# Five more filler matmuls after each of six mode pairs, and where the TensorE instruction fetches then fall

## The chip, the cores and the metric

The kernel runs on one core of one Trainium2 chip. The metric is device time in microseconds (us) of one execution; the profile's span, first to last instruction, is some 1.8 us shorter. All executions here are of the state that the harness calls fast.

## The reference, cut to what matters

```python
# linear attention with elu+1 features; q, k, v are 8 x 8 heads x 576 x 64
kv = einsum('bhsd,bhse->bhde', phi(k), v);  z = phi(k).sum(axis=2)
x  = (phi(q) @ kv) / (phi(q) . z + 1e-6)          # 8 x 576 x 512
# spectral mixing: 64 modes, one complex 512 x 512 weight for each
X = rfft(x, axis=1)[:, :64]
Y = X * (w_r + i w_i), mode by mode               # 64 x 2 x 1 MiB of float32 weights
u = x + irfft(Y, n=576)
out = u + relu(u @ w_ch)                          # 8 x 576 x 512 float32
```

The mode weights are 134 MB of float32 in memory, converted to bfloat16 on the way in. They set the length of the kernel.

## The kernel before: the parts that matter

The 64 modes are worked off in 32 pairs. Each pair needs two loads, one of w_r and one of w_i, into one of two buffers. GpSimd issues the load for pair p+2 when the products of pair p have read their buffer.

```python
def w_load(p, half, pool, tag, bufs):
    if half == 0:
        w_in[p] = pool.tile([128, NDW, D], BF16, tag=tag, bufs=bufs, name=f"w{p}")
    two = (moe_w_r, moe_w_i)[half][2 * p : 2 * p + 2]
    pin(nc.gpsimd.dma_start(out=w_in[p][half::2], in_=two.rearrange(...)))

def keep_warm(n):                       # a filler: a matmul whose result nobody reads
    for _ in range(n):
        pin(nc.tensor.matmul(last_ps[0], id16, wch16[:, 0, :]))

def mode_pair(p):
    w = w_get(p)                        # from pair 5 on: two buffers
    ...
    for dc in range(NDW):               # 16 products, wait for both loads
        product(P, xz[p % 2][:, dc]..., 32, w, dc, NDW)
    if p + 1 < LAST:
        set_diagonal(p + 1)
    st = evacuate(p, P)                 # VectorE or ScalarE
    work_slot(p, "mid")                 # other work, spread over the pairs
    picks(2 * p, st, 2)
    if p % 4 == 3:
        ...                             # VectorE moves a finished octet of modes
    work_slot(p, "end")
    keep_warm(FILL.get(p, 0))

FILL = {**{p: 7 for p in range(18, 27)}, 27: 9, 28: 5, 29: 6, 30: 4}
... # cut: attention, transforms, inverse transform and the output, see the whole kernel
```

After pair 30 comes the last pair. Its last loads arrive in pieces, each multiplied as soon as it is there (the tile y_last). The rows that come of it are copied into YZ_all by DMA, and the inverse transform, the rectifier, the sum and the stores follow from there.

Of the kernel before, what the change touches and what calls it, by code (L numbers as in the profile page):

```python
# [43 lines left out]
def kernel(  # L44
# [370 lines left out]
    def keep_warm(n: int):  # L415

        for _ in range(n):
            pin(nc.tensor.matmul(last_ps[0], id16, wch16[:, 0, :]))  # L418
# [4 lines left out]
    def work_slot(p: int, name: str):  # L423
        for _ in range(slots.get((p, name), 0)):
            if work:
                work.pop(0)()
# [34 lines left out]
    def mode_pair(p: int):  # L461
# [19 lines left out]
        work_slot(p, "end")  # L481
        keep_warm(FILL.get(p, 0))

# [47 lines left out]


    n_early = n_keep + n_pre
    FILL = {**{p: 7 for p in range(18, 27)}, 27: 9, 28: 5, 29: 6, 30: 4}
    ystage = ctx.enter_context(tc.tile_pool(name="ystage", bufs=1, side="right"))
    inv_sb = ystage.tile([2 * NM, S], F16, name="inv_sb")
    inv2_sb = ystage.tile([128, S], F16, name="inv2_sb")
# [474 lines left out]
```

## Time and profile before

| | before |
|---|---|
| time, median of the first 3 executions | 421.37 us (421.35 to 421.74) |
| span of the profiled execution | 419.6 us |
| TensorE busy, instructions traced | 288.7 us, 3115 matmuls and 3115 weight loads |
| last weight landing | 387.97 us |
| last y_last product ends | 388.27 us |
| last store landed | 418.41 us |

The page cuts the span into 40 slices of 10.5 us. The digits are tenths: TensorE's busy share, its granted clock, and the busy share of the DMA engines.

```profile
PE   0359799899517553444343685998798878899993
PEclk9999958989655555555555589799899989999997
DMA  8999999999999999999999999999999999998698
```

The DMA row is nines from the second to the 36th slice: a stream that never pauses. TensorE's clock is halved from the 12th to the 23rd slice, where it has little to do. The change puts fillers into part of that stretch.

A DMA transfer runs on 16 engines, and the trace has one landing record for each. The spread between the first and the last of the 16 tells how far the slowest engine is behind.

### The profile page before, as it was taken

How to read it: one execution, taken by the hardware profiler on the slowest of the kernel's cores; microseconds unless marked ns; L12 is line 12 of the kernel's file. 1: busy time of each engine (PE TensorE's matmuls, PEld its weight loads, DVE VectorE, ACT ScalarE, POOL GpSimd, SP SyncE). 2: the span in 40 equal slices, each digit the busy share in tenths (PEclk: the TensorE clock that was granted, in tenths of full speed). 3: DMA queues.
4: the chain of work that ended last, by engine and by line, in shares of the span. 5: the costliest groups of instructions: out<-in, count | busy, mean ns of one | idle time of the engine just before them, and what ended most of it. 6: DMA issues, size and time to landing. Idle time of an engine off the chain costs nothing.

```text
span 419.6 us, 7400 instructions
## 1 busy us (share of the span) xinstructions
PE 288.7 (69%) x3115; PEld 155.9 (37%) x3115; DVE 228.6 (54%) x499; ACT 154.2 (37%) x253; POOL 58.1 (14%) x100
## 2 busy tenths in 40 slices
PE   0359799899517553444343685998798878899993
PEld 0247677787301221222121232433343324354421
DVE  4587979994404462464645353454455433512794
ACT  4677888954101011000000233344253422230782
POOL 4222224210001111111111111111111111130000
PEclk9999958989655555555555589799899989999997
DMA  8999999999999999999999999999999999998698
GB/s 219 211 212 216 210 221 206 229 206 222 222 217 212 213 223 211 216 222 209 220 220 205 225 220 205 225 215 209 224 217 208 225 216 209 223 205 162 230 395 328
DMA packets 17073, 93.17 MB, mean 222 GB/s; under 512 B 2112, under 2 KB 3024, under 8 KB 12880
## 3 DMA queue, kind: packets, MB, share of 16 engines
q0 software_dynamic: 12496, 81.48, 93.3%
q1 hardware_dynamic: 4544, 11.22, 7.2%
q8 instruction: 24, 0.39, 0.3%
q14 instruction: 9, 0.07, 0.0%
HBM read 163.93 MB, written 9.44 MB: 413 GB/s over the span
## 4 chain that ended last, share of the span: by engine, by line
DMA 65%; PE 19%; DVE 5%; issue 3%; ACT 3%; POOL 2%; DVEq 0%; ACTq 0%; POOLq 0%
DMA w<-in_moe_w_i_dram 52%; DMA pick_sb<-row_pick 8%; PE P L431 7%; DMA k<-in_k_dram 5%; PE acc L747 3%; PE acc L787 2%; PE kvp L256 2%; ACT ke L207 2%; POOL w L116 2%; PE eps L688 1%; DVE x L292 1%; DVE ke L220 1%; POOL w L128 1%; DVE k L214 1%; PE zl L418 0%
## 5 line engine op out<-in xcount | busy, mean ns | idle before, releaser
L431 PE MATMUL P<-w,xz 128*32 128x512 bf16 x496 | 48.3, 530 | 64.3 <-DMA w<-in_moe_w_i_dram 61.8
L448 ACT CAST ys<-P 128x512 f16<-128x512 f32 x15 | 8.8, 585 | 131.6 <-PE P L431 131.6
L116 POOL DMA_DIRECT2D w<-in_moe_w_r_dram x31 | 17.8, 575 | 244.2 <-PE P L431 240.7
L431 PEld LDWEIGHTS <-xz 128*32 128x32 bf16 x496 | 13.2, 115 | 85.5 <-DMA w<-in_moe_w_i_dram 56.9
L446 DVE CAST ys<-P 128x512 f16<-128x512 f32 x17 | 11.8, 691 | 53.5 <-PE P L431 53.5
L688 PE MATMUL eps<-wch,xTw 128*128 128x512 f16 x144 | 40.6, 409 | 0.0
L162 PEld LDWEIGHTS <-qT 64*128 64x128 f16 (+1 forms) x640 | 22.8, 124 | 31.7 <-issue 17.2
L671 ACT CAST x16w<-x_main 128x512 f16<-128x512 f32 x32 | 19.8, 618 | 37.7 <-DVE x_main L669 37.7
L669 DVE TENSOR_TENSOR x_main<-ya,x_main 128x512 f32<-128x512 f32 x32 | 22.0, 691 | 18.7 <-PE ya L665 18.5
L256 PE MATMUL kvp<-vpad,ke 32*128 32x130 f16 x576 | 23.3, 255 | 9.1 <-ACT qT L243 6.4
L441 DVE COPY xz<-xt_c 64x256 bf16<-64x256 bf16 x62 | 22.9, 370 | 12.1 <-PE P L431 11.3
L696 ACT CAST E<-eps 128x512 f16<-128x512 f32 (+1 forms) x40 | 21.2, 539 | 19.5 <-PE eps L688 19.5
L256 PEld LDWEIGHTS <-ke 32*128 32x128 f16 x576 | 21.4, 113 | 10.8 <-issue 8.9
L162 PE MATMUL nw<-kv,qT 64*128 64x65 f16 (+1 forms) x320 | 18.9, 240 | 9.5 <-DVE x_tail L632 4.5
L418 PE MATMUL zl<-wch,id 128*128 128x512 f16 x93 | 23.0, 380 | 0.0
L292 DVE TENSOR_TENSOR x<-num,rd 128x512 f16<-128x512 f32 x32 | 22.1, 692 | 1.1
L236 PE MATMUL qTp<-id,qe 128*128 128x128 f16 x144 | 14.3, 278 | 11.7 <-DVE qe L220 9.5
L632 DVE TENSOR_TENSOR x_main<-nw,rd 128x256 f32<-128x256 f32 x32 | 11.2, 417 | 17.3 <-PE nw L162 17.3
L207 ACT ACTIVATE qe<-q 128x1152 f16<-128x1152 f16 (+1 forms) x16 | 17.9, 1157 | 7.5 <-DMA q<-in_q_dram 7.4
L454 PE MATMUL yt<-pick_sb,ys 128*128 128x32 f16 (+1 forms) x128 | 8.8, 186 | 16.9 <-DMA pick_sb<-row_pick 10.7
L680 DVE COPY xTw<-xTp 128x512 f16<-128x512 f16 x36 | 15.0, 416 | 10.0 <-PE xTp L678 9.9
L243 ACT COPY qT<-qTp 128x1152 f16<-128x1152 f16 x16 | 19.6, 1291 | 0.5 <-PE qTp L236 0.2
(118 smaller groups left out, 494.6 us busy)
## 6 DMA issues: line engine op xcount, KB each, us to landing
w<-in_moe_w_r_dram POOLq DMA_DIRECT2D x31, 1024.0 KB, 12.5
w<-in_moe_w_i_dram POOLq DMA_DIRECT2D x31, 1024.0 KB, 16.7
out_dram<-x_main SPq DMA_DIRECT2D x12, 512.0 KB, 3.8
k<-in_k_dram POOLq DMA_DIRECT2D x8, 576.0 KB, 13.1
v<-in_v_dram POOLq DMA_DIRECT2D x8, 576.0 KB, 14.4
q<-in_q_dram POOLq DMA_DIRECT2D x7, 576.0 KB, 12.8
out_dram<-x_main SPq DMA_DIRECT2D x8, 256.0 KB, 3.8
q<-in_q_dram SPq DMA_DIRECT2D x2, 576.0 KB, 4.5
```

The source lines that it names most:

```text
L116: nc.gpsimd.dma_start(out=w_in[p][half::2], in_=two.rearrange("g (r dc) e -> (g r) dc e", dc=NDW))
L162: mm = nc.tensor.matmul(num[hpo][orow, c0 : c0 + 65], qT[rows, hpp, h2, cols], kv_sb[rows, hpp, h2, :])
L207: pin(nc.scalar.activation(out=ev[:, c], in_=heads(nm, b, c), func=AF.Exp))
L256: nc.tensor.matmul(kv_ps[:, h2, 0:130], phi["k", b][r0 : r0 + 32, j // NJ, j % NJ].rearrange("p o d -> p (o d)"), vp[r0 : r0 + 32, :, j, 0 ...
L292: nc.vector.tensor_tensor(out=dst.rearrange("p (o c d) -> p o c d", o=2, c=4), in0=nv[:, :, :, 0:64], in1=rden.unsqueeze(3).broadcast_to([ ...
L418: pin(nc.tensor.matmul(last_ps[0], id16, wch16[:, 0, :]))
L431: nc.tensor.matmul(P[c : c + n, :], x, w[:, dc, :], start=(dc < NDC), stop=(dc >= n_dc - NDC), tile_position=(0, c), skip_group_check=True,)
L441: pin(nc.vector.tensor_copy(out=xz[p % 2][HALVES[h], :, h, :], in_=src))
L669: pin(nc.vector.tensor_tensor(out=x, in0=acc, in1=x, op=ALU.add))
L671: pin(nc.scalar.copy(out=x16w[t], in_=x))
L688: nc.tensor.matmul(e_ps, xT[:, c, :], wch16[:, c, :], start=(c == 0), stop=(c == NDC - 1))
L696: pin(nc.scalar.copy(out=dst, in_=e_ps[:, cols]))
```

## The change

The intent is in the title: 30 more fillers, five after each of the pairs 5 to 10 (modes 10 to 21). They need 60 more TensorE instructions (a weight load with each matmul), so every later 256-instruction block of TensorE's program is fetched that much earlier in the work.

```diff
-    FILL = {**{p: 7 for p in range(18, 27)}, 27: 9, 28: 5, 29: 6, 30: 4}
+    FILL = {**{p: 5 for p in range(5, 11)}, **{p: 7 for p in range(18, 27)}, 27: 9, 28: 5, 29: 6, 30: 4}
```

## The prediction

> **What bounds the kernel now.** I read the page's slices first, then sums by window, then the chain of waits over the stage that is changed, then the landing records of the single transfers. The times before are 421.35 to 421.74 us, median 421.37, and the profiled execution spans 419.6 us.
>
> The windows cut the run at the stages. The columns are busy time of each engine with its instruction count, then the granted TensorE clock, the DMA share and GB/s.
>
> ```profile
> 112.00:136.00 24.00, 10.34 (x96) 3.15 (x96) 6.32 (x15) 1.17 (x2) 2.23 (x4) 0.50 1.03 214
> 144.00:231.00 87.00, 37.54 (x474) 17.40 (x475) 43.98 (x148) 4.25 (x10) 9.78 (x18) 0.50 1.01 216
> 250.00:378.00 128.00, 106.59 (x772) 48.43 (x772) 55.42 (x114) 46.03 (x85) 16.86 (x31) 0.95 1.01 216
> 378.00:392.00 14.00, 13.15 (x126) 6.86 (x127) 5.24 (x12) 2.97 (x7) 1.11 (x2) 1.00 0.62 121
> 392.00:418.00 26.00, 20.45 (x109) 5.85 (x107) 21.24 (x21) 17.68 (x33) 0.00 (x0) 0.93 1.00 381
> ```
>
> From 144 to 231 us, the stage that the change touches, TensorE is busy 37.54 of 87 us at half clock. From 250 to 378 it is busy 106.59 of 128 us at 0.95 of the clock. The DMA share is 1.01 and the rate 216 GB/s in both. So the pace up to 378 us is the weight stream's, whatever TensorE's clock. The chain of waits says the same for this stage (start, length, what):
>
> ```profile
> 156.55 16.61 DMA w<-in_moe_w_i_dram
> 173.16 0.04 issue
> 173.21 1.93 PE P L431 x16
> 175.13 0.29 issue
> 175.42 0.54 POOL w L116
> 175.96 16.63 DMA w<-in_moe_w_i_dram
> ```
>
> A mode pair's 16 products start when its second load has landed (173.21), their end lets GpSimd issue the load two pairs ahead, and that takes 16.63 us because the other buffer's load is ahead of it. Two pairs take 19.4 us, one 9.7. With one load always still queued, shortening the 1.93 us of products issues the next load earlier but does not make the stream faster.
>
> The list of waits gives TensorE's slack:
>
> ```profile
> PE P L431 <- DMA w<-in_moe_w_i_dram: 61.8, 20, 5.8
> ```
>
> In the changed stage it idles 2.98 to 5.77 us ahead of each of the pairs 7 to 11, and 3.37 us ahead of pair 6.
>
> **Why instruction fetches could matter.** The queue table shows them:
>
> ```profile
> q0 software_dynamic: 12496, 81.48, 93.3%
> q1 hardware_dynamic: 4544, 11.22, 7.2%
> q8 instruction: 24, 0.39, 0.3%
> q14 instruction: 9, 0.07, 0.0%
> ```
>
> Queue 8 has 24 packets of 16,384 bytes. In the trace their starts follow TensorE's instruction count: 246 at the first, then about 256 apart (4310 at the 17th, 5869 at the 23rd, 6063 at the 24th). So they are TensorE's. Each takes 0.89 to 1.04 us on one DMA engine, and their durations repeat in a cycle of eight, so I infer that they go round eight engines.
>
> Each transfer posts 16 landings, and I read the time between the first and the last. It is 0.4 us up to 25 us, 1.5 after fetch 1, 2.6 after fetch 9 (94.61 us) and 3.7 after fetch 17 (255.23 us). The fetches between those bring other engines up to the slowest and add almost nothing to the last landing. So the first fetch of each round of eight costs the stream about 1.05 us and the other seven cost nothing. At the end of the loads (last landing 387.97 us) the slowest engine is 3.76 us behind the fastest.
>
> **What the Trainium skill says.**
> - "Runtime: NRT & Kernel Launch", section "Instruction fetch mechanics": instructions come in 16 KiB blocks of 256 by a DMA of the sequencer's own, TensorE holds 128 KiB, and a block crossing is mostly hidden. The trace agrees on block size and spacing. It shows no TensorE gap that a fetch ended, but a hidden cost of about 1 us per round in the weight stream.
> - "DMA: Bandwidth & Descriptors", section "Why a DMA increments its semaphore by 16 and not by 1": the 16 engines finish independently, and only the full 16 mean landed. The trace agrees (spreads of 0.4 to 3.8 us), so a wait is for the slowest engine.
> - "TensorE: Matmul & The Clock Gate", section "What's actually happening": the clock is halved unless TensorE was busy through a window of about 3.4 us. The trace agrees roughly: one unbroken half-clock stretch of 133 us, from 111 to 244 us, where TensorE has gaps of 3 to 6 us.
>
> **The change part by part.**
> 1. Added: 5 matmuls in each of the pairs 5 to 10, 30 in all. The order of instructions shows 6292 rows on TensorE against 6232, 60 more (a weight load with each), none more on another engine, and no transfer more.
> 2. Their time: the group of fillers, id times wch into zl, shows seven in 1.69 us at full clock, so five take 1.2 us, and at half clock at most 2.4. They come after a pair's other work, and the least wait after them is 2.98 us (ahead of pair 7). Left over: 0.6 us or more. They are wholly hidden: 0 us on the path.
> 3. The clock: busy time per pair goes from about 4.2 to 6.0 or 6.6 us of 9.7. That may give some full-clock windows between 145 and 195 us. Products then take 1.05 us (as at 290.65) in place of 1.90. The load two pairs ahead is issued 0.85 us earlier into a queue that holds another 9.7 us pair: 0 us.
> 4. Shifted fetches: fetch 13 comes about 30 instructions earlier in the work, fetch 14 some 50 or 60, all later ones 60, half a pair. Fetch 17 moves from 255 to about 251 us, fetch 23 from 381.95 to about 379. Both are in the stream before and after. Fetch 17 costs its 1.05 us either way, and fetch 23 nothing, as its engine was 1.2 us ahead of the slowest. There is no extra round: a 25th fetch would be due near instruction 6320 or later, and TensorE ends at 6246 plus 60.
> 5. Fetch 24, the one that changes phase: before, it starts at 396.42 us, amid the output stores (DMA share 1.00 from 392). The stores' spread goes from 0.8 to 2.0 us there. 60 instructions earlier is about 389 to 391 us, between the last weight landing (387.97) and the first stores (392), where the DMA engines are idle. Its lag of about 1.2 us on one engine is saved, but it has shrunk by the end: in the last store (418.41) three engines land 0.00, 0.09 and 0.10 us before the last, the others 0.35 to 0.53. The other two lag by what looks like queue 14's fetches at 403.53 and 407.31, which stay. So the end gains 0 to 0.1 us.
>
> The sum: 0 + 0 + 0 - 0.05 us, from 421.37 to about 421.3 us.
>
> **The rivals.**
> - Fetch 24 collides with the copy of the last rows into YZ_all. That is issued at 390.3 and 390.6 and lands at 393.54 and 394.47, and a TensorE product that reads it starts at 394.48. There is no slack, and the tail is dense on TensorE (10.00 of the 10 us from 400 to 410). A fetch at 391 to 393 on one engine could delay this by up to 1.0 us: 421.7 to 422.4. Against it: the estimate puts the fetch mostly ahead of 391. This is the main risk upward.
> - The store stream is bound by its slowest engine, not by what TensorE produces. Then moving fetch 24 away saves its whole 1.0 us: 420.4. For it: 381 GB/s and a share of 1.00 in this stage. Against it: the lag of that engine shrinks from 1.2 to about 0.4 us by itself, so the stores are waiting for data.
> - The warm clock speeds the stage. If TensorE paced the pairs, 0.85 us for each of six pairs would save 5 us: 416. Against it: pairs take 9.7 us at half clock and also at full clock (319.87 to 329.57).
> - The fillers delay products: six times 0.5 us would make 424. Against it: the slack above, and behind it the second buffer.
>
> **Range and chances.** Base 421.3. The YZ_all collision (one chance in five) adds 0.3 to 1.0 us. A store stream bound by its slowest engine (one in five) takes off 0.3 to 1.0. Runs of before spread over 0.4 us. So 420.6 to 422.0 holds 8 in 10. Two per cent is 8.4 us; none of the mechanisms with evidence reaches that.
>
> **What would show it.** Right: the same DMA share and 9.7 us per pair from 144 to 231 us. A last weight landing within 0.3 us of 387.97. 24 packets on queue 8, the 24th near 390 and the spread of the stores after 396 under 1 us. TensorE's waits ahead of the pairs 6 to 11 shorter by the fillers. Wrong: pairs longer than 9.75 us (fillers not hidden), a fourth step in the spread of landings (a 25th fetch, or a different engine), YZ_all landing after 394.6, or an end that moves with the stores' spread.

## The result, and the profile after

The changed kernel took 421.93 us (median of 6, 421.32 to 423.11). The kernel before took 421.38 us (421.28 to 421.74, 6 runs). The ratio is 1.0013, with a 95% interval of 0.9998 to 1.0027. A ratio here is the mean time of one kernel's fast runs over that of the other's of the same rounds (of the last job see below), so not quite the ratio of the medians. The verdict at 2% is "same", and the median lies in the predicted range. But it is 0.6 us above the predicted 421.3, and three of the six executions are over 422 us (long ones; those under 422 us are short). That is what the experiments are about.

First the stage that was changed. The windows have the same columns as in the prediction:

```profile
144.00:231.00 87.00, 48.57 (x499) 20.39 (x500) 44.03 (x148) 4.25 (x10) 9.76 (x18) 0.52 1.01 216
250.00:378.00 128.00, 105.80 (x762) 47.70 (x764) 55.47 (x114) 45.43 (x83) 16.81 (x31) 0.93 1.01 215
```

TensorE is busy 11 us more from 144 to 231 us, and the DMA share and the rate are what they were. The clock went from 0.50 to 0.52, one full-clock window of 3.4 us. The waits of the products for the loads between 143 and 194 us (total, count, longest) are, before:

```profile
PE P L431 <- DMA w<-in_moe_w_i_dram: 25.3, 6, 5.8
```

and after:

```profile
PE P L431 <- DMA w<-in_moe_w_i_dram: 12.2, 6, 3.6
```

13.1 us less over six pairs: the five fillers took 2.2 us a pair out of time in which TensorE waited anyway.

The fetches, from the trace, with the spread of the landings after each:

| fetch of TensorE instructions | before, us | after, us | what it did |
|---|---|---|---|
| 16 | 228.62 | 226.21 | nothing: spread 2.7, after 2.4 |
| 17, first of the third round | 255.23 | 250.31 | spread to 3.7 (before) and 3.4 (after), 1 us more in both |
| 23 | 381.95 | 379.99 | nothing on the last landing |
| 24, last | 396.42, amid the stores | 390.42, ahead of the stores | spread of the stores then 2.0 (before), 0.8 (after) |

The last weight landing is at 387.95 us, against 387.97. So the weight stream is as long as before. The span is still 0.8 us longer (420.3 against 419.6). The chain of waits says where that comes from. Before, from 371 us on (start, length, what):

```profile
371.91 14.79 DMA w<-in_moe_w_i_dram
386.71 0.05 issue
386.75 0.36 PE y_last L512 x8
387.11 0.23 PE zl L418
```

and after, the end of the same stretch:

```profile
385.37 0.59 PE P L431 x8
385.96 0.54 PE acc L787 x2
386.50 0.55 PE acc L880 x2
387.05 0.19 PE yt L454 x4
387.24 0.66 PE zl L418 x3
387.91 0.39 PE y_last L512 x16
```

Before, the chain goes back to the last load: TensorE was waiting for it. After, it goes back along TensorE alone: the pieces were there and TensorE was behind. The last y_last product ends at 389.13 us (before 388.27), and from there everything is 0.8 us later, the last store too (419.18 against 418.41). TensorE was behind because its clock was halved twice late in the run, from 351.3 to 358.1 and from 364.9 to 371.8 us. The slices show it in the clock row from the 34th to the 36th place:

```profile
PE   0369998999617775665343668888788877999993
PEclk9999998579855556555555598999999997889998
DMA  8999999999999999999999999999999999997698
```

Before, the clock was full from 342.9 to 414.6 us.

### The profile page after: what moved, and what is told of

It is laid out like the page before. It is cut to its first block, busy times and chain, and to the rows that moved or that the text cites. A ratio compares the mean times of both kernels' runs of the same rounds, so it can differ in the third digit from the quotient of the medians.

```text
span 420.3 us, 7460 instructions
## 1 busy us (share of the span) xinstructions
PE 304.5 (72%) x3145; PEld 161.2 (38%) x3145; DVE 229.5 (55%) x499; ACT 154.2 (37%) x253; POOL 57.4 (14%) x100
## 4 chain that ended last, share of the span: by engine, by line
DMA 62%; PE 26%; DVE 3%; ACT 3%; issue 2%; POOL 2%; DVEq 0%; POOLq 0%; ACTq 0%
DMA w<-in_moe_w_i_dram 49%; DMA pick_sb<-row_pick 8%; PE P L431 7%; DMA k<-in_k_dram 5%; PE acc L747 3%; PE z L710 2%; PE zl L418 2%; PE acc L787 2%; PE kvp L256 2%; POOL w L116 2%; ACT ke L207 1%; PE xf L354 1%; PE yp L723 1%; ACT qT L243 1%; PE qTp L236 1%
## 5 line engine op out<-in xcount | busy, mean ns | idle before, releaser
L431 PE MATMUL P<-w,xz 128*32 128x512 bf16 x496 | 46.9, 516 | 51.8 <-DMA w<-in_moe_w_i_dram 49.4
L418 PE MATMUL zl<-wch,id 128*128 128x512 f16 x123 | 38.9, 461 | 0.0
L688 PE MATMUL eps<-wch,xTw 128*128 128x512 f16 x144 | 38.0, 388 | 0.0
L162 PE MATMUL num<-kv,qT 64*128 64x65 f16 (+1 forms) x320 | 16.5, 219 | 5.4 <-DVE x L292 3.0
## 6 DMA issues: line engine op xcount, KB each, us to landing
w<-in_moe_w_r_dram POOLq DMA_DIRECT2D x31, 1024.0 KB, 13.1
```

Source lines behind the costliest of these rows:

```text
L162: mm = nc.tensor.matmul(num[hpo][orow, c0 : c0 + 65], qT[rows, hpp, h2, cols], kv_sb[rows, hpp, h2, :])
L431: nc.tensor.matmul(P[c : c + n, :], x, w[:, dc, :], start=(dc < NDC), stop=(dc >= n_dc - NDC), tile_position=(0, c), skip_group_check=True,)
L688: nc.tensor.matmul(e_ps, xT[:, c, :], wch16[:, c, :], start=(c == 0), stop=(c == NDC - 1))
```

## The experiments

The question: does the change slow the kernel (by its fetches or by its fillers), or did the clock, whose checks fall differently in each execution, make half of these executions late?

**The kernel before, again, as it stands.**

> The kernel before once more, unchanged, for its spread and for a second trace. Theory 1 (the clock's window, which falls differently in each execution, decides how late TensorE is at the last load): this kernel shows the same spread as the changed one if it is run often enough, so some executions of 422 us or more, and a ratio to itself of 0.999 to 1.001. Theory 2 (the change itself costs about 0.5 us): all executions stay within 421.2 to 421.8 us. Last weight landing at 387.9 to 388.1 us in the trace either way.

Measured: 424.21, 421.30, 421.55, 421.45, 421.42 and 422.22 us, ratio to its own runs 1.0011 (0.9991 to 1.0030). So the kernel before has long executions too, and compared with itself it can show about the ratio that the change showed. The profiled execution was the one of 424.21 us. Two windows of it, with the columns as before:

```profile
359.00:366.00 7.00, 6.48 (x38) 2.38 (x30) 2.84 (x5) 1.17 (x2) 1.09 (x2) 0.53 1.05 222
366.00:373.00 7.00, 7.00 (x20) 1.94 (x20) 2.40 (x5) 2.34 (x4) 0.00 (x0) 0.50 1.03 220
```

The clock was halved from 359.4 to 373.0 us. TensorE did 20 matmuls between 366 and 373 us. In the first profile of the same kernel it was:

```profile
366.00:373.00 7.00, 6.91 (x76) 4.59 (x75) 1.71 (x5) 2.93 (x5) 3.24 (x6) 1.00 1.04 220
```

76 in the same 7 us. Pair 29's products started at 373.44 us (first profile 368.39), and the last y_last product ended at 390.92 us, 2.1 us after the last landing. The span is 422.4 us, and from 378 us to the end of y_last the chain of waits runs along TensorE alone. The last landing was late too (388.81 us), so the expectation that put it at 387.9 to 388.1 in every case was wrong. The trace points to a fetch: a late TensorE fetches late, and fetch 23 came at 386.59 us (first profile 381.95). The first six pieces of the last loads landed within 0.2 us of the first profile's times, the two behind that fetch 1.0 and 0.84 us later, with the spread up from 1.1 to 2.1 us.

**The changed kernel, again.**

> The changed kernel once more, unchanged. Theory 1: a median within 0.3 us of the kernel before in the same rounds, or of its copy. Theory 2: a ratio of 1.001 to 1.002 again with an interval clear of 1. In the trace: last weight landing within 0.1 us of 387.95; if the clock is granted in full from 340 to 390 us, the last y_last product ends near 388.3 us and the span is 419.4 to 419.6; if it is halved within 340 to 375 us, it ends later and the span is longer by as much.

Measured: 421.96 us median, 421.22 to 423.27, three of six over 422; ratio 1.0014 (0.9998 to 1.0030), so not clear of 1 as theory 2 had it; but the median is 0.45 us above the 421.51 of the kernel before in these rounds, more than the 0.3 us that theory 1 allowed. Neither forecast was met. The profiled execution is a short one (span 419.8 us). Its clock was full from 255.6 to 416 us, the last landing was at 388.11 and the last y_last product ended at 388.41. With the clock up, the changed kernel is as quick as the kernel before.

**The same shift of the fetches, without the fillers' time.**

```diff
+    def small_fill(n: int):
+        for _ in range(n):
+            pin(nc.tensor.matmul(last_ps[0][0:32, 0:16], id16[:, 0:32], wch16[:, 0, 0:16]))
 ...
         keep_warm(FILL.get(p, 0))
+        small_fill(SMALL.get(p, 0))
 ...
+    SMALL = {p: 5 for p in range(5, 11)}
```

> Five matmuls of 16 columns in the place of the five fillers of 512 in each of the modes 10 to 21's pairs: the same 60 instructions and so the same shift of the fetches, but next to no TensorE time. If the shifted fetches cost something (theory 2a), this shows what the changed kernel shows, 421.9 us and the stores' spread after 396 us under 1 us. If the fillers' time and the clock do (theory 2b), it is at 421.4 us. Theory 1: 421.3 to 422 us, with fetch 24 near 389 to 391 us and nothing gained by it beyond 0.1 us.

Measured: 422.38, 421.28, 424.07, 424.06, 422.24 and 421.29 us; ratio 1.0024 (1.0001 to 1.0047). The median of 422.31 is above all three forecasts, and the interval just leaves out 1. The profiled execution was a long one: clock halved from 351.9 to 358.7 and from 365.6 to 372.4 us, last landing 387.93, TensorE 1.5 us behind at the end of y_last. Fetch 24 came at 390.97, and the stores' spread then was 0.75 to 0.9 us. The two short executions are as short as any of the kernel before. So neither the shifted fetches nor the fillers' time lengthens a short execution. The long one that was traced is of the same kind as before. Four of six is more than the kernel before has; this is taken up below.

**A fourth round of fetches inside the weight stream.** The same small matmuls, 30 after each of the pairs 6 to 14.

```diff
+    SMALL = {p: 30 for p in range(6, 15)}
```

> 270 matmuls of 16 columns, 540 instructions, spread over the pairs 6 to 14: two blocks and a little more, so that the 25th fetch, the first of a fourth round of eight engines, comes ahead of the last weight landing (near 379 us). If the first fetch of a round costs the stream 1.05 us: fetch 25 is seen before 388 us, the spread of the landings takes a fourth step to about 4.6 to 4.8 us, the last weight landing is at 388.9 to 389.1 us in place of 387.97 and the time is 422.2 to 422.6 us. If a fetch costs nothing in the stream: last landing 387.97, time 421.4 us.

Measured: fetch 25 at 381.82 us. The queue table now has

```profile
q8 instruction: 26, 0.43, 0.4%
```

and the landings read:

| weight transfer that landed last at | spread of its 16 landings |
|---|---|
| 380.69 us (before fetch 25) | 3.83 us |
| 384.05 us | 4.74 us |
| 388.91 us (the last one) | 4.59 us |

The fourth step is there, and the last landing is 0.94 us later than 387.97. In that execution TensorE was on time, and the last store landed 0.87 us later than in the first profile of before. The short ones of the six are 422.12, 422.20 and 422.47 us, as expected; three more at 423.1 to 423.7 put the median at 422.78, above what was expected; ratio 1.0029 (1.0017 to 1.0042). So in these traces a fetch's cost to the stream depends on whether its engine is already the slowest.

**Fillers where TensorE idles late, to hold the clock.** Pair 27 has waits of 0.69, 0.78 and 0.52 us inside it and 2.0 us after it.

```diff
         work_slot(p, "mid")
+        keep_warm(MID.get(p, 0))
         picks(2 * p, st, 2)
 ...
+        keep_warm(MID.get(p, 0))
         work_slot(p, "end")
 ...
+    FILL |= {24: 12, 25: 13, 26: 9, 27: 15}
+    MID = {27: 3}
```

> The kernel before, with fillers where TensorE idles between 320 and 359 us: 5 more after pair 24, 6 after 25, 2 after 26, 6 after 27, and 3 ahead of and 3 behind pair 27's picks, each set shorter than the wait that it fills (the waits are 1.75, 2.11, 0.70, 2.00, 0.69 and 0.78 us at full clock; a filler takes 0.24 us). Theory 1 (executions over 422 us come from a window of little TensorE work near 348 to 359 us, after which the clock is halved and TensorE is late at the last load): no or nearly no execution over 421.9 us, median 421.3 to 421.5 us, clock full from 345 to 390 us in the trace. Rival (the long executions come from something else, the fetches or the memory): one in four or more over 422 us as with the changed kernel, or lateness with the full clock.

Measured: 421.46 us median, five of six between 421.24 and 421.55, one of 422.34; ratio 0.9992 (0.9972 to 1.0012). The kernel before had five of eleven over 422 us in the same job (up to 424.00). The profiled execution had the full clock from 306 to 415 us.

**The same on top of the change.**

> The changed kernel (five fillers in each of the modes 10 to 21's pairs) with the same further fillers as warm_late. Theory 1: the same as warm_late within 0.2 us, all executions under 421.9 us, so that the change itself does nothing. If the shifted fetches cost something of their own: 0.3 us or more above warm_late, with long executions left.

Measured: 422.24 to 422.85 us, all six, median 422.51; ratio 1.0014 (0.9995 to 1.0034). Both theories missed this: hardly any spread, but all executions 1 us longer. The trace explains it. TensorE was on time (y_last done at 388.46, copy into YZ_all issued at 390.49, in warm_late 390.36), and yet the last store landed at 419.80 us (warm_late 418.59). The queue table has one packet more:

```profile
q8 instruction: 25, 0.41, 0.4%
```

The 30 fillers of the change and the 25 of this experiment together bring TensorE to 6342 instructions, against 6292 in the changed kernel, and cross the next block. Fetch 25 came at 411.86 us, 2.5 us before the last store was issued. The spread of the stores' landings went from 0.8 us (landed 412.33) to 2.05 us (414.88) and was still 1.78 us at the last store, where warm_late has 0.43 us. The store instructions were issued at the same times within 0.1 us. From the end of y_last to the last landing it takes 31.34 us, against 30.25 in warm_late. So the trace puts this 1.1 us down to one engine's fetch that nothing behind it could absorb; no run moved that fetch alone.

**TensorE late on purpose.** Nine more fillers behind pair 30.

```diff
-    FILL = {..., 27: 9, 28: 5, 29: 6, 30: 4}
+    FILL = {..., 27: 9, 28: 5, 29: 6, 30: 13}
```

> The kernel before with 9 more fillers behind pair 30, so that TensorE alone is late by 9 x 0.235 = 2.1 us for the last pair, with the clock full and all loads as before. In the trace of before it has about 1.0 us to spare there (in the changed kernel's trace, 1.9 us late at the last pair gave 0.86 us at the last y_last product). Expected: last weight landing still at 387.97 us, last y_last product about 1.1 us later than 388.27, the copy into YZ_all and the end later by the same: 422.4 to 422.6 us. If TensorE's lateness does not carry through to the end: 421.4 us.

Measured: 422.08, 422.17, 422.19, 422.21, 424.34 and 425.73 us; ratio 1.0028 (0.9998 to 1.0059). The four shortest are 0.8 us over the short ones of before (median 421.39), somewhat less than the 1.1 us expected. The last landing was at 387.93 us. So TensorE's lateness at the last pair does carry through to the end, after some 1.3 us that it has to spare (2.1 us added, 0.8 seen). The profiled execution was a long one, with the halved clock on top (351.7 to 358.5 and 365.4 to 372.2 us).

**How often: both kernels and the warmed one again.** Same kernels, more executions.

> The changed kernel a third time, to count its long executions. Theory 1 in its plain form (chance alone): about as many over 422 us as the kernel before has in the same job. If the change makes them more likely: 6 of 12 so far, so 2 to 4 of 6 here, against 3 of 23 of the kernel before so far.

Measured: 421.37, 422.93, 421.44, 421.45, 422.01 and 423.03 us; ratio 1.0003 (0.9980 to 1.0025). Three of six over 422 us, the kernel before five of eleven beside it.

> The kernel before once more, with the job's own runs of it: 17 more executions, to settle how often it goes over 422 us (8 of 34 so far). If the change makes long executions no more likely, about a third here as well, near what aa_after3 shows; if the changed kernel is really worse, a fifth or fewer.

Measured: 422.27, 421.10, 421.85, 421.28, 421.38 and 421.11 us; ratio 0.9986 (0.9965 to 1.0008). The 17 new executions that were hoped for became 7: of the eleven runs of the kernel before that this job lists, ten stand with the same times in the job before, so only 421.14 is new. One of seven was long, which the expectation had as the sign that the changed kernel is really worse. The ratios of this run and of the next three mostly compare with runs of the job before. The profiled execution was the long one. It looks like the first profile of the changed kernel: clock halved from 351.3 to 358.1 and from 364.9 to 371.8 us, y_last done at 389.09, last landing 387.95, span 420.5 us.

> The changed kernel a fourth time: 9 of 18 executions over 422 us so far. Chance alone: about the same share as the kernel before in this job, and the short executions of both at 421.2 to 421.7 us. The change at work: 3 or more of 6 over 422 us, against a fifth of the kernel before.

Measured: 421.28, 423.08, 421.97, 421.14, 422.05 and 422.04 us; ratio 1.0000 (0.9978 to 1.0022). Three of six were long beside one of seven of the kernel before: the forecast for "the change at work", where aa_after2 had come out as chance would.

> warm_late once more (1 of 6 over 422 us before, where the kernel before had 5 of 11 in the same job). If the fillers near 348 to 359 us keep the clock up: at most 1 of 6 over 422 us, median 421.3 to 421.5. If that was luck: as the kernel before.

Measured: 421.17 to 421.65 us, all six, as expected if the fillers keep the clock up; ratio 0.9989 (0.9969 to 1.0008).

**The warmed kernel without the five fillers behind pair 28.**

```diff
-    FILL = {..., 27: 9, 28: 5, 29: 6, 30: 4}
+    FILL = {..., 27: 9, 28: 0, 29: 6, 30: 4}
```

> warm_late without the five fillers behind pair 28, which take 1.25 us at full clock and 2.3 us at half clock just ahead of the last loads. If the clock stays up: same as warm_late, with about 1.3 us more idle ahead of pair 29. If it is halved there: TensorE is 2.3 us earlier for pair 29 than in the long traces so far, so lateness at the last y_last product under 0.3 us and no execution over 422 us. Against it: the idle time itself may let the clock fall at 368 to 375 us, and then executions over 422 us stay.

Measured: 421.17 to 421.49 us, all six, median 421.29; ratio 0.9985 (0.9963 to 1.0006). Its profile, in the two windows where the others lose the clock:

```profile
348.00:352.00 4.00, 3.61 (x33) 1.41 (x33) 0.69 (x1) 0.59 (x1) 1.08 (x2) 1.00 0.98 209
352.00:359.00 7.00, 5.78 (x46) 2.93 (x46) 2.99 (x6) 0.59 (x1) 0.00 (x0) 1.00 1.05 222
```

and the first profile of the changed kernel:

```profile
348.00:352.00 4.00, 1.83 (x24) 0.86 (x24) 0.69 (x1) 0.59 (x1) 1.08 (x2) 0.91 1.00 213
352.00:359.00 7.00, 6.48 (x28) 2.59 (x26) 2.96 (x6) 0.59 (x1) 0.00 (x0) 0.56 1.01 215
```

TensorE is busy 1.83 of the 4 us about the loss, and 3.61 with the fillers. In the next window 28 matmuls take 6.48 us at the half clock, where in warm_trim 46 take 5.78. The short execution of aa_after kept its clock, with 1.83 us between 348 and 352 as well. But these windows were cut by hand. All clock changes of one execution lie multiples of 3.41 us apart, so they mark a grid, and on that grid the two differ. The last window ahead of the loss in the first profile of the changed kernel, and the one at the same place in aa_after, are:

```profile
347.90:351.31 3.41, 1.69 (x22) 0.62 (x20) 0.30 (x1) 0.59 (x1) 0.98 (x2) 1.00 1.04 221
347.79:351.20 3.41, 1.95 (x23) 0.71 (x21) 0.04 (x1) 0.58 (x1) 0.71 (x2) 1.00 0.99 211
```

The other traces without late fillers agree: 1.45 to 1.75 us in the window ahead of a loss at 351 to 352 us (aa_before2, shift_only, aa_after2, late_tensor), 1.41 and 1.44 us ahead of one at 359 us (aa_before, aa_after3), and 1.93 or 1.94 us where the clock was kept around 349 to 353 us (before, aa_before, aa_after3). With the late fillers TensorE is busy 2.71 us or more in every window from 340 to 374 us. So the work there is close to what decides, and a small shift of the grid tips it. It is not the whole rule. aa_after also kept its clock after a window with 1.53 us (337.55 to 340.96), and the second loss of the long execution, at 365 us, came after one with 2.90 us (361.55 to 364.97), where aa_after with 2.89 us kept it. What decides there is open.

**All executions together.**

| kernel | executions | short (under 422 us): median | 422 us and over |
|---|---|---|---|
| before (all jobs, and its two copies) | 41 | 421.39 | 9 |
| changed | 24 | 421.39 | 12 |
| shift_only | 6 | 421.29 | 4 |
| warm_late, both times | 12 | 421.44 | 1 |
| warm_trim | 6 | 421.29 | 0 |

Left out are round4, late_tensor and warm_late_changed, which are all over 422 us for reasons given above. The short executions of the two kernels do not differ. What is **shown** is the kind of the long ones. Only 4 of the 25 long executions of a kernel without added work late in the run were traced: the changed kernel's first, shift_only's and both copies of before. All four have the clock halved for 13.7 us in total between 351 and 373 us, and TensorE behind at the end of y_last by 1.1 to 2.1 us. None of the traces of short executions has more than 6.8 us of halved clock there (aa_after2, 352.1 to 358.9, still on time), and in all of them the last y_last product ends 0.3 us after the last landing.

What is **not settled** is whether the change makes the long ones more likely. 12 of 24 against 9 of 41 would come up by chance about 3 times in 100 if the rates were equal, and shift_only points the same way. But this hangs on the cut: three of the 12 lie at 422.01 to 422.05 us, and with a cut at 422.1 us it is 9 of 24 against 9 of 41, which chance gives about 25 times in 100. And the rate of the kernel before itself was 0 of 6, 3 of 17, 5 of 11 and 1 of 7 from job to job, while the changed kernel had 3 of 6 each time. I found no path by which a fetch or a filler before 195 us would reach the clock at 350 us: with the clock up, both kernels start pair 26's products at the same time within 0.01 us (339.28 and 339.27). Nor is it shown that the warmed kernels beat the kernel before. Their intervals contain 1, and 1 long execution of 18 against 9 of 41 is too few to be sure.

## Why the prediction was right or wrong

- **The bound (right, with a gap).** The stream sets the pace to 378 us: share 1.01 and 216 GB/s in both. But "whatever TensorE's clock" failed at the end of the stream. TensorE has 1.0 to 1.3 us to spare at the last pieces, and 13.7 us of half clock between 351 and 373 us use that up and more. This is the step that failed: the sum had no term for the clock late in the run, as I asked for its effect only in the stage that was changed.
- **The fillers' time (right).** At most 2.4 us a pair and hidden; 2.2 measured, all of it out of waits.
- **The clock in the changed stage (right).** One full-clock window from 160.1 to 163.5 us, and no pair quicker for it. The fillers are not what made it: aa_before2, late_tensor and shift_only, without their time, have such a window at 157 to 161 us too.
- **The shifted fetches (right).** 24 packets; fetch 17 at 250.31 us, 1 us of spread, as before; fetch 23 at 379.99 without effect; last landing 387.95. round4 then made the first fetch of a round come once more in the stream, and it cost 0.94 us where 1.05 was expected. That the other seven cost nothing holds only while their engines are ahead: in aa_before fetch 23 fell on the last two pieces and made them 1.0 and 0.84 us later. No 25th fetch in the changed kernel; at 50 instructions more (warm_late_changed) it was there.
- **Fetch 24 (right).** Expected at 389 to 391 us, seen at 390.42, and the stores' spread after 396 us stayed under 0.9 us until 400 us (then 1.06 us once, at 406.76, after a fetch of queue 14 at 404.39). The expected gain of 0 to 0.1 us: from the end of y_last to the last store landing it takes 30.14, 30.34 and 30.25 us in the three traces of before and 30.05, 30.24, 30.03 and 30.04 us in the four of the changed kernel. That is 0.15 us less on average, at the edge of what such few traces tell.
- **The rivals.** The collision with the copy into YZ_all didn't happen: it landed 0.84 us later (395.31), but it was issued 0.85 us later, by a late TensorE; so the sign "after 394.6" came from another cause. warm_late had the collision: fetch 24 came at 391.51 us and lasted 1.63 us, and the two copies took 4.40 and 4.87 us in place of 3.24 and 3.90. TensorE waited 0.19 us for the first of them, and from the end of y_last to the last store it took 30.25 us, as in before. So "there is no slack" was misread: in warm_late the first product that reads YZ_all starts at 394.81 us, after the first copy (394.76) and ahead of the second (395.51), and in the kernel before that first copy has 0.9 us to spare. That the stores are bound by their slowest engine is wrong for a fetch at 396 us, whose lag shrinks in the 20 us that follow, and right for one at 411.86 us (1.1 us). The fillers delayed no products, and the warm clock sped up nothing.
- **The number.** 421.3 fits the short executions (421.39). The median of 421.93 counts three long ones of six. The range was built on "runs of before spread over 0.4 us", which were three executions; 41 spread over 3.1 us. The range held the result partly by luck: the changed kernel's last six executions have a median of 422.01 us, just outside it. And for the upper half of it the reason that I gave was not the one at work.

The skill's page "TensorE: Matmul & The Clock Gate", section "What's actually happening", also says that the window of about 3.4 us runs free and does not restart with the kernel. (Its table has the halved clock as the default and as what follows an idle window; the prediction's "unless TensorE was busy through a window" runs the two together.) The traces agree on the free-running window: each clock change lies a multiple of 3.41 us from the others of its execution, and the same loss falls at 351.3, 351.7, 351.9, 352.1, 359.1 or 359.4 us, or not at all, in different executions. That is the lottery.

## What to carry to other kernels

Time the kernel before against itself before reading a ratio of 1.001, and look at one long and one short execution: here they differed in the TensorE clock, not in anything that the change had moved. Read a clock loss against the work on the grid that the clock changes mark, not in windows cut by hand. Where a stream sets the pace, ask for the slack of the other engines at its end, with their clock halved. And count instructions in blocks of 256: a fetch is free in most places, but costs about 1 us on one DMA engine when that engine is already the slowest or when the kernel is about to end.

## What the Trainium skill lacked or had wrong

- "Runtime: NRT & Kernel Launch", section "Instruction fetch mechanics", calls a block crossing mostly hidden. That holds for TensorE's waits. It lacks that the 16 KiB occupy one DMA engine for 0.89 to 1.04 us (1.63 us for the one amid warm_late's copies), that the fetches go round what the landings show as eight engines, and that the first of each round lengthens a saturated stream by about 1 us (0.94 us in round4, at 381.82 us) while the other seven do not as long as their engines are ahead (aa_before's fetch 23, at 386.59 us, was not free); and that with a fetch 8 us before the end of the stores the kernel took 1.1 us longer.
- "TensorE: Matmul & The Clock Gate", section "HAM oscillation — how this bites in real kernels", gives as the rule that there be no idle gaps over about 3.4 us. Here the clock was halved at 351.3 us amid gaps of 0.70, 0.69 and 0.78 us, after a window of 3.41 us in which TensorE was busy 1.69 us; with 1.95 us at the same place it was kept (aa_after). The same page also tells of a kernel whose short idles made the clock swing, but gives no measure of how much work is enough. Nor do these traces give a rule: elsewhere 1.53 us were enough, and 2.90 us were not.
- No page says that the engines of a saturated stream keep their lag: in the kernel before, the slowest stayed 3.7 to 3.8 us behind the fastest from 261 to 388 us, apart from one transfer right after a fetch (4.4 us).
